# Rows 128 to 179 of the inverse transform two blocks at a time, and a wider spacing of Z in memory

## The chip, the cores and the metric

The kernel runs on one core of a Trainium2 chip. The metric is device time in microseconds (us), lower is better. A run's time is that of the whole program; the profiler recorded one execution.

## The reference

Inputs are x of shape [8, 5696, 128], a filter h of [5696, 128], complex mode weights w_r + i w_i of [64, 128, 128] and w_ch of [128, 128], all float32. A causal long convolution is followed by a mixing of the lowest 64 modes and a small pointwise layer:

```python
L = 2 * S
a = irfft(rfft(x, n=L, axis=1) * rfft(h, n=L, axis=0), n=L, axis=1)[:, :S]   # convolution
X = rfft(a, axis=1)
Y = zeros_like(X)
Y[:, :64] = einsum('bmd,mde->bme', X[:, :64], w_r + 1j * w_i)                # mode mixing
u = a + irfft(Y, n=S, axis=1)
out = u + maximum(u @ w_ch, 0)
```

## The kernel before

The transform of length 2S is split as time = 64 q + p, with 89 values of q (NQ) and 64 of p (J), and 90 frequency classes k (NK). Batches are taken in pairs, g = 0 to 3.

**First part, per pair.** A first transform over q fills As; then come "ticks" of four classes each (`tick`, NT = 23 a pair). A tick multiplies As with the matrix M (`second`, matmuls on 64 rows that alternate between partitions 0-63 and 64-127, one for each batch), multiplies by the filter's spectrum Hs (U), transforms back over the 64 points with Wc, and evacuates the result Z into Zs or Zt. From there SyncE writes Z to a scratch tensor in memory, `zscr` (512 bytes a packet, ring "z"). Matmuls of Z with G sum the modes on the side.

**Last part.** For each pair of batches Z comes back from memory with (k, real or imaginary) on the partitions: 180 rows. A block is 16 of the 64 positions p, so there are 4 blocks a pair of batches and 16 in all, numbered i. `load_zt(i)` makes two DMAs of a block: rows 0-127 into buffer ZT..a, rows 128-179 (52 of them) into ZT..b, where they stand on partitions 32-83; `clear_zt` sets partitions 0-31 of that buffer to zero on GpSimd. There are five such buffer pairs (NC = 5), laid over memory that the first part no longer uses, and block i+5 is loaded when block i has been used up. The first four blocks are loaded from within the last pair's ticks, by the table `early`.

`u_tile(i, b, half)` makes 8 positions of one batch b in two PSUM banks. For each bank there is one matmul of the mixed modes (`u_c`, IBs with C, 356 columns) and for each of 4 positions two matmuls of 89 columns, S4a with ZT..a on 128 rows and S4b with ZT..b on 84 rows. S4a and S4b are tables of cosines and sines; only half of each is loaded, and `reflect` fills the rest from it (S4a on VectorE, S4b on ScalarE). ScalarE or VectorE then copies the two banks into u (UT).

`o_tile` makes 512 output rows a time: four matmuls of u with WI = [w_ch, identity], a RELU by ScalarE into R, an addition by VectorE into an output buffer (O, 7 buffers that hold two tiles each, and 4 small ones, Os), and a DMA to the output by SyncE (ring "o"). u-tiles and o-tiles share four pairs of PSUM banks in turn (LSLOT). The loops interleave them: for the first pair of batches there are u-tiles alone, for later ones 1 and 2 o-tiles of the earlier pair after the u-tiles in turn; in the last pair all of batch 0 comes before batch 1, with 2 or 3 o-tiles after each u-tile.

Before C is known, some u-tiles of block 0 are begun "ahead" (`u_z(..., alone=True)`), between the parts of the mode mixing `mix`.

Every engine works its instructions in the order in which they are recorded; waits are derived from the buffers. All DMAs of the last part except two small ones are issued by SyncE, so a load that must wait for its buffer holds up what SyncE has after it.

Of the kernel before, what the change touches and what calls it, by code (L numbers as in the profile page):

```python
# [4 lines left out]
P = 128  # L5
# [118 lines left out]
def bass_long_conv_fft__then__afno_spectral_mix_kernel(nc, x, h, moe_w_r, moe_w_i, moe_w_ch, out):  # L124
# [3 lines left out]
    J = 64  # L128
# [33 lines left out]
    s4t = np.zeros((P, 2 * SH))  # L162
    s4t[:, 0:SH] = rows[0:P, 0:SH]
    s4t[PB:PB + RB, SH:2 * SH] = rows[P:2 * NK, 0:SH]
    sg = np.ones((P, 3))
    sr = np.stack([(-1.0) ** kk, -(-1.0) ** kk], axis=1).reshape(2 * NK)
    sg[:, 0] = sr[0:P]
    sg[PB:PB + RB, 1] = sr[P:2 * NK]
    sg[M:P, 2] = -1.0
    tt = np.arange(S)  # L170
# [79 lines left out]
    wc_sb = at("Wc", 2 * P, F16, take(2 * P * 2))  # L250
    sg_sb = at("SG", 3, F32, take(12))
# [4 lines left out]
    ZB = 16  # L256
# [4 lines left out]
    zt_off = [(a_h, a_h2), (a_as1, a_as1 + 2 * ZP), (a_as1 + 4 * ZP, a_as1 + 6 * ZP), (a_h + 2 * ZP, a_h2 + 2 * ZP),  # L261
              (a_m2, a_g)]
    assert 2 * S + 8 * ZP <= AW * 2
    zt = [[at(f"ZT{i}{'ab'[p_]}", ZP, F16, zt_off[i][p_]) for p_ in range(2)] for i in range(NC)]
    ib_sb = at("IBs", S, F16, a_m)
    s4_sb = [at("S4a", S, F16, a_m + 2 * S), at("S4b", S, F16, a_as)]
    assert 4 * S + 2 * ZP + 4 * P + 2048 <= 2 * MW
# [259 lines left out]
    ZX = [("zs", i, b) for i in range(NZ, NZL) for b in range(2)]  # L527
    zt_old = [(H_ALL, H_ALL), (AST, AST), (AST, AST), (H_ALL, H_ALL), (M_ALL[3:6], G_ALL)]

    def load_zt(i):  # L530
        g_, c_ = divmod(i, J // ZB)
        for part, (p0, r0, n) in enumerate(((0, 0, P), (PB, P, RB))):
            old = list(once(("zt", i % NC, part), zt_old[i % NC][part]))
            dma("sync", bass.AP(zt[i % NC][part], p0 * ZP, [[ZP, n], [1, ZP]]),
                bass.AP(zs, (g_ * 2 * NK + r0) * J * 256 + c_ * ZB * 256, [[J * 256, n], [1, ZP]]),
                "t", [("zd", g_, s_) for s_ in range(NT)], [("zt", i % NC, part)], after=old)

    def clear_zt(i):
        z32 = zt[i][1][0:PB, :].bitcast(U32)
        R.add("gpsimd", lambda e: e.memset(z32, 0), (), [("zt0", i)], after=list(zt_old[i][1]) + pace)  # L540

    def load_ib():
# [11 lines left out]
    def load_s4(part):  # L554
        n = PB + RB if part else P
        dma("sync", s4_sb[part][0:n, 0:SH], bass.AP(c_s4, part * SH, [[2 * SH, n], [1, SH]]), "p", (),
            [("s4", part, 0)], after=AST if part else M_ALL[1:4])
# [5 lines left out]
    early = {3: lambda: load_w(2), 5: lambda: load_w(3), 8: lambda: load_s4(1),  # L563
             9: lambda: clear_zt(0),
             10: lambda: load_zt(0),
             12: lambda: load_s4(0),
             14: lambda: (load_id(), load_ib(), clear_zt(1)),
             16: lambda: load_zt(1),
             19: lambda: (load_zt(3), clear_zt(3)),
             NT - 2: lambda: (load_zt(2), clear_zt(2))}  # L570
    pace = []

# [91 lines left out]
    def tick(g_, t):  # L664
# [27 lines left out]
        if LC <= t < NT + LC:  # L692
            s_ = t - LC
            n = len(ticks[s_])
            i, zi = s_ % NU, zroom(g_, s_)
            zb = [turns("z", ZBANK) for b in range(2)]
            for b in range(2):
                for r in range(2):
                    mm(pv(zb[b], 0, [[1, n * D]]), (W1, W2)[r], u_s[i][:, r * 1024 + b * 512:r * 1024 + b * 512 + n * D],
                       r == 0, r == 1, [("u", i), ("wc",)], [bank(zb[b])])  # L700
                evac(bass.AP(z_s[zi], b * D, [[1024, P], [2 * D, n], [1, D]]),
                     pv(zb[b], 0, [[D, n], [1, D]]), [bank(zb[b])], [("zs", zi, b)], eng="scalar",
                     after=once(("zx", zi, b), Z_OLD) if zi >= NZ else ())
                if b == 0:
                    drained(g_, t, 0)
            zo = (g_ * NK + KT * s_) * P * 256
            dma("sync", bass.AP(zs, zo, [[256, P], [P * 256, n], [1, 256]]),
                bass.AP(z_s[zi], 0, [[1024, P], [256, n], [1, 256]]), "z",
                [("zs", zi, 0), ("zs", zi, 1)], [("zd", g_, s_)])
# [39 lines left out]
    for g_ in range(NP):  # L749
# [3 lines left out]
        for t in range(NT + LM):  # L753
            tick(g_, t)
            assert g_ + 1 < NP or not wp
            if g_ == NP - 1 and t in early:
                pace[:] = [("u", min(t, NT - 1) % NU)]
                early[t]()
# [13 lines left out]

    pace[:] = []
    load_wi()
    for i in range(4, NC):
        load_zt(i)
        clear_zt(i)

# [4 lines left out]

    def u_z(i, b, half, alone=False, parts=(0, 1)):
        g_, c_ = divmod(i, NCH)
        t = ahead.get((i, b, half))
        if t is None:
            t = turns("l", LSLOT)
        z = zt[i % NC]
        for hb in parts:  # L790
            if not alone:
                u_c(i, b, half, t, hb, True)
            for pl in range(4):
                for ri in range(2):
                    pz = half * 8 + hb * 4 + pl
                    so = (c_ * ZB + pz) * NQ
                    n = (P, PB + RB)[ri]
                    mm(pv(t + hb, pl * NQ, [[1, NQ]]), z[ri][0:n, pz * 256 + b * P:pz * 256 + b * P + P], s4_sb[ri][0:n, so:so + NQ],
                       alone and pl == 0 and ri == 0, not alone and pl == 3 and ri == 1, [("zt", i % NC, ri), ("zt0", i % NC), ("s4", ri, 0)] + ([("s4", ri, 1)] if c_ >= NCH // 2 else []), [bank(t + hb)])
        if alone:  # L800
            ahead[(i, b, half)] = t
        return t

    def u_c(i, b, half, t, hb, first_):
        g_, c_ = divmod(i, NCH)
        pl0 = half * 8 + hb * 4
        mm(pv(t + hb, 0, [[1, 4 * NQ]]), c_sb[:, (2 * g_ + b) * P:(2 * g_ + b + 1) * P],
           ib_sb[:, (c_ * ZB + pl0) * NQ:(c_ * ZB + pl0 + 4) * NQ], first_, not first_,
           [("c", g_ // 2), ("ib", 0)] + ([("ib", 1)] if c_ >= NCH // 2 else []), [bank(t + hb)])

    def u_tile(i, b, half):
        g_, c_ = divmod(i, NCH)
        t = ahead.get((i, b, half))
        if t is None:
            t = u_z(i, b, half)
        else:
            for hb in range(2):
                u_c(i, b, half, t, hb, False)
        ub = (g_ % 2) * 2 + b
# [3 lines left out]
        src = pv(t, 0, [[1, NQ], [512, 2], [NQ, 4]])  # L823
        evac(bass.AP(u_sb[ub], c_ * ZB + half * 8, [[S, P], [J, NQ], [4, 2], [1, 4]]),
             src, [bank(t), bank(t + 1)], [("u_", ub, 2 * c_ + half)], eng=e, after=once(("u", ub), old))
# [32 lines left out]
    reflect("vector", ib_sb, P, 2, ("ib",), M_ALL[0:2])  # L858

# [52 lines left out]
    todo = []  # L912
    NB = NCH * NP
    NW4 = NW // 4
    for g_ in range(NP):
        last = g_ == NP - 1
        order = [(c_, b) for b in range(2) for c_ in range(NCH)] if last else [(c_, b) for c_ in range(NCH) for b in range(2)]
        for n, (c_, b) in enumerate(order):
            i = NCH * g_ + c_
            for half in range(2):  # L920
                u_tile(i, b, half)
                for _ in range((2, 2 + half)[n >= NCH] if last else 1 + half):
# [4 lines left out]
            if last and n == NCH - 1:  # L927
                todo += [(g_, 0, r4) for r4 in range(NW4)]
# [37 lines left out]
```

## Time and profile before

| | |
|---|---|
| median of 3 runs | 372.04 us (370.41 to 372.57) |
| span of the profiled execution, first to last instruction | 370.1 us |
| TensorE (PE) busy | 354.7 us, 96% |
| ScalarE (ACT) busy | 316.2 us, 85% |
| VectorE (DVE) busy | 291.8 us, 79% |
| GpSimd (POOL) busy | 75.2 us, 20% |
| granted TensorE clock | 0.999 |
| moved by DMA | 103.94 MB |

The profiled execution's own time is told by its span; the runs' times include what lies around that. In the profile a line of the grouping gives engine, operation, what is written and read, shapes and count, then busy time, the mean of one in ns, and idle time before it. L323 is the helper through which all matmuls pass, L320 that of all DMAs, so that groups are told apart by their tiles. Matmuls are pipelined: the duration of one is longer than the step from one to the next.

### The profile page before, as it was taken

The numbers are of one execution on the slowest core, as the hardware profiler recorded it, in microseconds if no ns is written. First come the engines' busy times: TensorE is split into PE (matmuls) and PEld (weight loads), VectorE is DVE, ScalarE is ACT, GpSimd is POOL, SyncE is SP. The second block draws the span as 40 slices with busy tenths as digits, with TensorE's granted clock in tenths as the row PEclk, the third lists the DMA queues.
The fourth block names the chain that finished last, engine by engine and source line by source line (L and its number), as shares of the span: only waits on it lengthen the run. The fifth ranks groups of instructions, "written<-read, shape, count | busy, mean of one in ns | idle before, by whom it ended". The sixth has DMA issues, their size and how long they took to land.

```text
span 370.1 us, 12455 instructions
## 1 busy us (share of the span) xinstructions
PE 354.7 (96%) x5350; PEld 276.5 (75%) x5350; DVE 291.8 (79%) x332; ACT 316.2 (85%) x499; POOL 75.2 (20%) x117
## 2 busy tenths in 40 slices
PE   7999899999999999999999999999999999999994
PEld 7878766667866668866668766668899888888873
DVE  3549899988999999989999988775357777756666
ACT  8559999999999999999999999995467777688885
POOL 8804012100833311823213001151000000000000
PEclk9999999999999999999999999999999999999999
DMA  7999979969999996999996999999999999999878
GB/s 139 209 271 382 249 165 292 232 198 283 93 140 213 263 258 186 132 160 215 263 278 128 171 310 363 342 345 388 381 410 386 413 410 408 418 399 376 326 291 349
DMA packets 87048, 103.94 MB, mean 281 GB/s; under 512 B 22730, under 2 KB 72522, under 8 KB 83438
## 3 DMA queue, kind: packets, MB, share of 16 engines
q1 hardware_dynamic: 64610, 81.33, 62.5%
q0 software_dynamic: 22384, 21.83, 35.4%
q8 instruction: 42, 0.69, 0.7%
q14 instruction: 12, 0.10, 0.1%
HBM read 70.61 MB, written 51.12 MB: 329 GB/s over the span
## 4 chain that ended last, share of the span: by engine, by line
PE 78%; ACT 10%; DMA 7%; DVE 3%; issue 1%; POOL 1%; DVEq 0%; POOLq 0%
PE ps L323 78%; ACT As L313 6%; DMA out_dram<-O 5%; DMA Hin<-in_h_dram 2%; ACT R L898 1%; DVE As L317 1%; ACT Xs L311 1%; DVE U L623 1%; POOL Hin L320 1%; ACT UT L311 1%; DVE O L899 0%; ACT Zs L311 0%; DVE Hp L438 0%; ACT C L313 0%; DVE Hs L315 0%
## 5 line engine op out<-in xcount | busy, mean ns | idle before, releaser
L652 DVE TENSOR_TENSOR U<-Xs,Hs 128x2048 f16<-128x2048 f16 (+1 forms) x72 | 85.8, 1197 | 12.1 <-ACT Xs L311 11.5
L323 PE MATMUL ps<-U,Wc 128*128 128x512 f16 (+1 forms) x368 | 93.8, 376 | 1.4 <-DVE U L623 1.4
L311 ACT CAST Xs<-ps 128x1024 f16<-128x1024 f32 (+1 forms) x76 | 75.0, 995 | 5.8 <-PE ps L323 3.1
L311 ACT CAST Zs<-ps 128x512 f16<-128x512 f32 (+1 forms) x132 | 70.1, 605 | 0.7
L899 DVE TENSOR_TENSOR O<-ps,R 128x512 f32<-128x512 f32 x81 | 52.4, 684 | 21.6 <-ACT R L898 11.4
L898 ACT ACTIVATE R<-ps 128x512 f32<-128x512 f32 (+1 forms) x92 | 50.5, 592 | 8.5 <-PE ps L323 8.4
L317 DVE TENSOR_SCALAR As<-ps 128x720 f16<-128x720 f32 x64 | 53.1, 879 | 4.8 <-PE ps L323 3.3
L323 PE MATMUL ps<-As,M 64*128 64x128 f16 (+3 forms) x1504 | 52.5, 214 | 2.4 <-ACT As L313 1.2
L313 ACT ACTIVATE As<-ps 128x720 f16<-128x720 f32 (+1 forms) x68 | 48.2, 771 | 5.0 <-PE ps L323 4.8
L323 PE MATMUL ps<-F,Xin 128*128 128x180 f16 x512 | 52.1, 249 | 0.1
L323 PE MATMUL ps<-WI,UT 128*128 128x256 f16 x360 | 50.8, 278 | 0.5 <-ACT UT L311 0.4
L311 ACT CAST UT<-ps 128x712 f16<-128x712 f32 x46 | 34.5, 752 | 19.4 <-PE ps L323 18.4
L323 PEld LDWEIGHTS ps<-U,Wc 128*128 128x128 f16 x368 | 29.1, 97 | 28.2 <-DVE U L623 1.9
L323 PEld LDWEIGHTS ps<-F,Xin 128*128 128x128 f16 x512 | 45.2, 155 | 6.7 <-DVE Xin L365 0.9
L323 PEld LDWEIGHTS ps<-As,M 64*128 64x128 f16 x1504 | 42.2, 94 | 8.7 <-ACT Xs L311 1.9
L323 PEld LDWEIGHTS ps<-WI,UT 128*128 128x128 f16 x360 | 38.9, 152 | 3.2 <-issue 1.8
L323 PE MATMUL ps<-IBs,C 128*128 128x356 f16 x128 | 39.2, 314 | 0.8 <-DVE O L899 0.7
L320 POOL DMA_DIRECT2D Xt<-in_x_dram x40 | 21.4, 540 | 76.5 <-PE ps L323 76.0
L323 PEld LDWEIGHTS ps<-G,Zs 128*128 128x128 f16 x512 | 26.1, 96 | 14.1 <-ACT Zs L311 0.2
L652 DVE TENSOR_TENSOR U<-ps,Hs 128x2048 f16<-128x2048 f32 (+1 forms) x16 | 35.5, 2216 | 0.0
L323 PE MATMUL ps<-G,Zs 128*128 128x128 f16 (+2 forms) x512 | 31.9, 192 | 0.1
L311 ACT CAST Zt<-ps 128x512 f16<-128x512 f32 x52 | 29.1, 659 | 0.0
(76 smaller groups left out, 479.4 us busy)
## 6 DMA issues: line engine op xcount, KB each, us to landing
out_dram<-O SPq DMA_DIRECT2D x39, 512.0 KB, 10.5
zscr<-Zs SPq DMA_DIRECT2D x62, 256.0 KB, 6.7
zscr<-Zt SPq DMA_DIRECT2D x26, 256.0 KB, 6.6
Xt<-in_x_dram POOLq DMA_DIRECT2D x20, 320.0 KB, 6.9
W<-wscr SPq DMA_DIRECT2D x4, 1024.0 KB, 8.5
ZT0a<-zscr SPq DMA_DIRECT2D x4, 1024.0 KB, 11.0
M<-cM POOLq DMA_DIRECT2D x5, 720.0 KB, 17.6
ZT1a<-zscr SPq DMA_DIRECT2D x3, 1024.0 KB, 11.1
```

Source lines behind the costliest of these rows:

```text
L311: R.add(e, lambda h_: h_.copy(dst, src), reads, writes, after=after)
L313: R.add(e, lambda h_: h_.activation(dst, src, COPY, scale=scale), reads, writes, after=after)
L317: R.add(e, lambda h_: h_.tensor_scalar_mul(dst, src, scale), reads, writes, after=after)
L320: R.add(eng, lambda h_: h_.dma_start(dst, src), reads, writes, ring=ring, after=after)
L323: R.add("tensor", lambda h_: h_.matmul(o, l, r, start=st, stop=sp), reads, writes)
L623: R.add("vector", lambda e: e.tensor_tensor(bass.AP(u_s[0], b * 512 + d0, [[2048, P], [1024, 2], [D, n], [1, d1 - d0]]), bass.AP(s_[0], s_ ...
L652: R.add("vector", lambda e: e.tensor_tensor(uv, src, hv, MULT), bk + [("h", t, 0), ("h", t, 1, 0), ("h", t, 1, J)], [("u", i)])
L898: R.add("scalar", lambda e: e.activation(rv, src_r, RELU), bk, [("r", i % NR)], after=once(("r", i % NR), G_ALL + XTT + [("y", 0), ("y", 1 ...
L899: R.add("vector", lambda e: e.tensor_tensor(ov, src_u, rv, ADD), bk + [("r", i % NR)], [key + (h_,)], after=once(key, old))
```

## The change

Rows 128-179 of two neighbouring blocks (2k and 2k+1) now share one buffer, ZB: the even block's on partitions 0-51, the odd block's on 64-115. S4b is laid out in the same way, for the even blocks on the lower and for the odd ones on the upper partitions, so that it has half the columns; it is loaded whole, and its reflection and the clears on GpSimd are gone. `u_tile(k, b, h4)` makes 4 positions of block 2k in one PSUM bank and the same 4 of block 2k+1 in the other. Its order is: both mode matmuls, eight matmuls on 128 rows, then eight on 52 rows that alternate between the lower and the upper partitions. There are 7 buffers for rows 0-127 (ZA) and 3 for the shared rows (ZB). Loads are issued at the end of a pair of blocks: both parts of ZB for pair k+3, then ZA for blocks 2k+7 and 2k+8. In memory the classes of Z are 69,632 bytes apart instead of 65,536. The number of matmuls, and the bytes of Z read and written, stay the same.

```diff
-    RB, PB = 2 * NK - P, 32
+    RB, PB = 2 * NK - P, 64
...
-    s4t[PB:PB + RB, SH:2 * SH] = rows[P:2 * NK, 0:SH]
+    s4b = np.zeros((P, S // 2))
+    for p0 in range(2):
+        s4b[p0 * PB:p0 * PB + RB] = rows[P:].reshape(RB, J // ZB // 2, 2, ZB * NQ)[:, :, p0].reshape(RB, S // 2)
+    s4t = np.concatenate([rows[0:P, 0:SH], s4b], axis=1)
...
-    zs = nc.dram_tensor("zscr", [NP * NK * P, 2 * D], F16, kind="Internal")
+    CS = P * 2 * D + 2048
+    zs = nc.dram_tensor("zscr", [NP * NK, CS], F16, kind="Internal")
...
-    NC = 5
+    NCA, NCB = 7, 3
...
-    def load_zt(i):
...
-    def clear_zt(i):
...
+    def load_za(i):
+        g_, c_ = divmod(i, J // ZB)
+        r_ = i % NCA
+        dma("sync", za[r_][:, :], bass.AP(zs, g_ * NK * CS + c_ * ZP, [[CS, P // 2], [J * 256, 2], [1, ZP]]),
+            "t", zdone(g_), [("za", r_)], after=once(("za", r_), za_old[r_]))
+
+    def load_zb(k):
+        r_ = k % NCB
+        for p0 in range(2):
+            g_, c_ = divmod(2 * k + p0, J // ZB)
+            n = RB - RS
+            dma("sync", bass.AP(zb_[r_], p0 * PB * ZP, [[ZP, n], [1, ZP]]),
+                bass.AP(zs, (g_ * NK + P // 2) * CS + c_ * ZP, [[CS, n // 2], [J * 256, 2], [1, ZP]]),
+                "t", zdone(g_), [("zb", r_, p0)], after=once(("zb", r_, p0), zb_old[r_]))
...
-             10: lambda: load_zt(0),
+             10: lambda: (load_za(0), load_zb(0)),
...
-             14: lambda: (load_id(), load_ib(), clear_zt(1)),
-             16: lambda: load_zt(1),
-             19: lambda: (load_zt(3), clear_zt(3)),
-             NT - 2: lambda: (load_zt(2), clear_zt(2))}
+             14: lambda: (load_id(), load_ib()),
+             16: lambda: load_za(1),
+             19: lambda: (load_za(2), load_zb(1)),
+             NT - 2: lambda: load_za(3)}
...
-    for i in range(4, NC):
-        load_zt(i)
-        clear_zt(i)
+    load_za(4)
+    load_zb(2)
+    load_za(5)
+    load_za(6)
...
+        if not alone:
+            for hb in range(2):
+                u_c(k, b, h4, t, hb, True)
+        for hb in range(2 if 0 in parts else 0):
+            z, r_ = za[(2 * k + hb) % NCA], (2 * k + hb) % NCA
             for pl in range(4):
...
+                mm(pv(t + hb, pl * NQ, [[1, NQ]]), z[:, pz * 256 + b * P:pz * 256 + b * P + P], s4_sb[0][:, so:so + NQ], ...)
+        for pl in range(4 if 1 in parts else 0):
...
+            for hb in range(2):
+                r0 = hb * PB
+                mm(pv(t + hb, pl * NQ, [[1, NQ]]), zb_[r_][r0:r0 + RB, pz * 256 + b * P:pz * 256 + b * P + P],
+                   s4_sb[1][r0:r0 + RB, so:so + NQ], ...)
...
-    reflect("scalar", s4_sb[1], PB + RB, 1, ("s4", 1), AST)
...
-            if b == 1 and i + NC < NB:
-                load_zt(i + NC)
+            if b == 1:
+                if k + NCB < NPR * NP:
+                    load_zb(k + NCB)
+                for i in (2 * k, 2 * k + 1):
+                    if i + NCA < NCH * NP:
+                        load_za(i + NCA)
```

More of the change, by code (lines that the diff above doesn't have):

```diff
@@ L250, in bass_long_conv_fft__then__afno_spectral_mix_kernel @@
     wc_sb = at("Wc", 2 * P, F16, take(2 * P * 2))
-    sg_sb = at("SG", 3, F32, take(12))
+    sg_sb = at("SG", 2, F32, take(8))
     XTW = 3 * M
@@ L260, in bass_long_conv_fft__then__afno_spectral_mix_kernel @@
     a_as1, a_m2 = a_as + 2 * S, a_m + 4 * S
-    zt_off = [(a_h, a_h2), (a_as1, a_as1 + 2 * ZP), (a_as1 + 4 * ZP, a_as1 + 6 * ZP), (a_h + 2 * ZP, a_h2 + 2 * ZP),
-              (a_m2, a_g)]
+    za_off = [a_h, a_as1, a_h + 2 * ZP, a_as1 + 4 * ZP, a_as1 + 6 * ZP, a_m2, a_g]
+    zb_off = [a_h2, a_h2 + 2 * ZP, a_as1 + 2 * ZP]
     assert 2 * S + 8 * ZP <= AW * 2
-    zt = [[at(f"ZT{i}{'ab'[p_]}", ZP, F16, zt_off[i][p_]) for p_ in range(2)] for i in range(NC)]
+    za = [at(f"ZA{i}", ZP, F16, za_off[i]) for i in range(NCA)]
+    zb_ = [at(f"ZB{i}", ZP, F16, zb_off[i]) for i in range(NCB)]
     ib_sb = at("IBs", S, F16, a_m)
-    s4_sb = [at("S4a", S, F16, a_m + 2 * S), at("S4b", S, F16, a_as)]
+    s4_sb = [at("S4a", S, F16, a_m + 2 * S), at("S4b", S // 2, F16, a_as)]
     assert 4 * S + 2 * ZP + 4 * P + 2048 <= 2 * MW
@@ L527, in bass_long_conv_fft__then__afno_spectral_mix_kernel, with zdone @@
     ZX = [("zs", i, b) for i in range(NZ, NZL) for b in range(2)]
-    zt_old = [(H_ALL, H_ALL), (AST, AST), (AST, AST), (H_ALL, H_ALL), (M_ALL[3:6], G_ALL)]
-    def load_zt(i):
-        g_, c_ = divmod(i, J // ZB)
[L532 to L536, printed above, removed]
-    def clear_zt(i):
-        z32 = zt[i][1][0:PB, :].bitcast(U32)
-        R.add("gpsimd", lambda e: e.memset(z32, 0), (), [("zt0", i)], after=list(zt_old[i][1]) + pace)
+    za_old = [H_ALL, AST, H_ALL, AST, AST, M_ALL[3:6], G_ALL]
+    zb_old = [H_ALL, H_ALL, AST]
+    def zdone(g_):
+        return [("zd", g_, s_) for s_ in range(NT)]
+    def load_za(i):
+        g_, c_ = divmod(i, J // ZB)
+        r_ = i % NCA
[9 more added lines that the diff above has]
+                "t", zdone(g_), [("zb", r_, p0)], after=once(("zb", r_, p0), zb_old[r_]))
     def load_ib():
@@ L554, in load_s4 @@
     def load_s4(part):
-        n = PB + RB if part else P
-        dma("sync", s4_sb[part][0:n, 0:SH], bass.AP(c_s4, part * SH, [[2 * SH, n], [1, SH]]), "p", (),
+        w = S // 2 if part else SH
+        dma("sync", s4_sb[part][:, 0:w], bass.AP(c_s4, part * SH, [[SH + S // 2, P], [1, w]]), "p", (),
             [("s4", part, 0)], after=AST if part else M_ALL[1:4])
@@ L782, in bass_long_conv_fft__then__afno_spectral_mix_kernel, with u_z @@
     ahead = {}
-    def u_z(i, b, half, alone=False, parts=(0, 1)):
-        g_, c_ = divmod(i, NCH)
-        t = ahead.get((i, b, half))
+    def u_z(k, b, h4, alone=False, parts=(0, 1)):
+        g_, c_ = divmod(2 * k, NCH)
+        t = ahead.get((k, b, h4))
         if t is None:
             t = turns("l", LSLOT)
[L789 to L792, printed above, removed]
-            for pl in range(4):
[L794 to L799, printed above, removed]
+        if not alone:
+            for hb in range(2):
+                u_c(k, b, h4, t, hb, True)
+        ns = [("s4", 0, 0)] + [("s4", 0, 1)] * (c_ >= NCH // 2)
+        for hb in range(2 if 0 in parts else 0):
+            z, r_ = za[(2 * k + hb) % NCA], (2 * k + hb) % NCA
+            for pl in range(4):
+                pz = h4 * 4 + pl
+                so = ((c_ + hb) * ZB + pz) * NQ
+                mm(pv(t + hb, pl * NQ, [[1, NQ]]), z[:, pz * 256 + b * P:pz * 256 + b * P + P], s4_sb[0][:, so:so + NQ],
+                   alone and pl == 0, False, [("za", r_)] + ns, [bank(t + hb)])
+        r_ = k % NCB
+        for pl in range(4 if 1 in parts else 0):
+            pz = h4 * 4 + pl
+            so = (c_ // 2 * ZB + pz) * NQ
+            for hb in range(2):
+                r0 = hb * PB
+                mm(pv(t + hb, pl * NQ, [[1, NQ]]), zb_[r_][r0:r0 + RB, pz * 256 + b * P:pz * 256 + b * P + P],
+                   s4_sb[1][r0:r0 + RB, so:so + NQ], False, not alone and pl == 3,
+                   [("zb", r_, hb), ("s4", 1, 0)], [bank(t + hb)])
@@ L800, in u_z, with u_c @@
         if alone:
-            ahead[(i, b, half)] = t
+            ahead[(k, b, h4)] = t
         return t
-    def u_c(i, b, half, t, hb, first_):
-        g_, c_ = divmod(i, NCH)
-        pl0 = half * 8 + hb * 4
+    def u_c(k, b, h4, t, hb, first_):
+        g_, c_ = divmod(2 * k, NCH)
         mm(pv(t + hb, 0, [[1, 4 * NQ]]), c_sb[:, (2 * g_ + b) * P:(2 * g_ + b + 1) * P],
-           ib_sb[:, (c_ * ZB + pl0) * NQ:(c_ * ZB + pl0 + 4) * NQ], first_, not first_,
+           ib_sb[:, ((c_ + hb) * ZB + h4 * 4) * NQ:((c_ + hb) * ZB + h4 * 4 + 4) * NQ], first_, not first_,
@@ L809, in u_c, with u_tile @@
            [("c", g_ // 2), ("ib", 0)] + ([("ib", 1)] if c_ >= NCH // 2 else []), [bank(t + hb)])
-    def u_tile(i, b, half):
-        g_, c_ = divmod(i, NCH)
-        t = ahead.get((i, b, half))
+    def u_tile(k, b, h4):
+        g_, c_ = divmod(2 * k, NCH)
+        t = ahead.get((k, b, h4))
         if t is None:
-            t = u_z(i, b, half)
+            t = u_z(k, b, h4)
         else:
             for hb in range(2):
-                u_c(i, b, half, t, hb, False)
+                u_c(k, b, h4, t, hb, False)
@@ L823, in u_tile @@
         src = pv(t, 0, [[1, NQ], [512, 2], [NQ, 4]])
-        evac(bass.AP(u_sb[ub], c_ * ZB + half * 8, [[S, P], [J, NQ], [4, 2], [1, 4]]),
-             src, [bank(t), bank(t + 1)], [("u_", ub, 2 * c_ + half)], eng=e, after=once(("u", ub), old))
+        evac(bass.AP(u_sb[ub], c_ * ZB + h4 * 4, [[S, P], [J, NQ], [ZB, 2], [1, 4]]),
+             src, [bank(t), bank(t + 1)], [("u_", ub, 2 * c_ + h4)], eng=e, after=once(("u", ub), old))
     XTT = [(n, g_) for g_ in range(NP) for n in ("xt", "xtn")]
     reflect("vector", s4_sb[0], P, 0, ("s4", 0), M_ALL[1:4])
-    reflect("scalar", s4_sb[1], PB + RB, 1, ("s4", 1), AST)
     MC = 4
@@ L916, in bass_long_conv_fft__then__afno_spectral_mix_kernel @@
         last = g_ == NP - 1
-        order = [(c_, b) for b in range(2) for c_ in range(NCH)] if last else [(c_, b) for c_ in range(NCH) for b in range(2)]
+        order = [(c_, b) for b in range(2) for c_ in range(NPR)] if last else [(c_, b) for c_ in range(NPR) for b in range(2)]
         for n, (c_, b) in enumerate(order):
[L919 to L922, printed above, removed]
+            k = NPR * g_ + c_
+            for h4 in range(4):
+                u_tile(k, b, h4)
+                for _ in range((2, 2 + h4 % 2)[n >= NPR] if last else 1 + h4 % 2):
                     if todo:
                         o_tile(*todo.pop(0))
-            if b == 1 and i + NC < NB:
-                load_zt(i + NC)
-            if last and n == NCH - 1:
+            if b == 1:
[4 more added lines that the diff above has]
+                        load_za(i + NCA)
+            if last and n == NPR - 1:
                 todo += [(g_, 0, r4) for r4 in range(NW4)]
```

22 lines of the change are left out of this document (8 added, 14 removed).

## The prediction

> **What bounds the kernel now.** I read the page's head first, then the busy times of four stretches of the last stage, then the chain that ended last, then the issues and landings of single DMAs.
>
> ```profile
> span 370.1 us, 12455 instructions
> PE 354.7 (96%) x5350; PEld 276.5 (75%) x5350; DVE 291.8 (79%) x332; ACT 316.2 (85%) x499; POOL 75.2 (20%) x117
> ```
> ```profile
> core 0: us, PE busy (x) PEld busy (x) DVE busy (x) ACT busy (x) POOL busy (x), PEclk, DMA share, GB/s
> 257.80:270.80 13.00, 12.97 (x239) 11.33 (x236) 4.78 (x6) 6.39 (x10) 0.00 (x0) 1.00 1.00 389
> 270.80:297.20 26.40, 26.40 (x381) 23.71 (x379) 19.00 (x28) 19.40 (x34) 0.00 (x0) 1.00 1.00 402
> 297.20:323.90 26.70, 26.43 (x378) 23.59 (x375) 19.31 (x29) 19.11 (x34) 0.00 (x0) 1.00 1.02 411
> 323.90:340.30 16.40, 15.81 (x209) 13.86 (x208) 9.64 (x16) 13.55 (x25) 0.00 (x0) 1.00 0.96 389
> ```
>
> The change touches only what begins when the last group of ticks ends (about 249 us); the windows start with the first tile that has all its operands. Two resources are full at once there. TensorE is busy 96 to 100% of each stretch, and up to 323.9 us the DMA engines are full too, at 389 to 411 GB/s. In one group of two batches the queue moves four blocks of Z (180 rows of 8 KB each, 5.9 MB) and 5.83 MB of output: 11.7 MB, 28.5 us at 411 GB/s, while the second and the third stretch, one group each, lasted 26.4 and 26.7 us. So the queue falls behind by about 2 us a group, and lives on the Z blocks that were fetched before output began.
>
> ```profile
> 262.63 54.98 PE ps L323 x816
> ...
> 320.68 16.68 DMA out_dram<-O
> ...
> 337.48 0.70 DVE O L899
> ...
> 338.32 7.48 PE ps L323 x100
> ```
> ```profile
> out_dram<-O SPq DMA_DIRECT2D x2, 512.0 KB, 12.4
> ...
> out_dram<-O SPq DMA_DIRECT2D x1, 512.0 KB, 15.6
> ```
>
> The chain is PE for 55 us, and then, once, a DMA: the output write issued at 320.68 lands 16.68 us later, VectorE at 337.48 fills the buffer that it frees, PE goes on at 338.32. The DMA view shows how that grew: 12.4 us from issue to landing for the writes issued in 297 to 304 us, 15.6 for that in 311 to 315, then the 16.68 of the chain. An output buffer can thus be away for about 16.7 us; beyond that PE waits one for one. The Z loads have as little slack there:
>
> ```profile
> 335.77 0.20 PE L323 MATMUL ps<-S4a,ZT0a 128*128 128x89 f16 x1
> 336.13 0.21 PE L323 MATMUL ps<-S4b,ZT0b 84*128 84x89 f16 x1 [0.16 <-DMA ZT0b<-zscr]
> ```
>
> Two neighbouring matmuls of block 15 start 0.36 us apart, the second released by the landing of ZT0b: a wait of 0.3 us.
>
> **PE: pairs and what frames them.**
>
> ```profile
> 257.82 0.31 PE L323 MATMUL ps<-IBs,C 128*128 128x356 f16 x1
> ...
> 258.31 0.32 PE L323 MATMUL ps<-IBs,C 128*128 128x356 f16 x1
> 258.47 0.20 PE L323 MATMUL ps<-S4a,ZT1a 128*128 128x89 f16 x1
> 258.51 0.20 PE L323 MATMUL ps<-S4b,ZT1b 84*128 84x89 f16 x1
> ```
>
> Half a u-tile before is one IBs matmul and eight Z matmuls, and the next IBs starts 0.49 us later. The IBs takes 0.16 of it (258.31 to 258.47), a Z matmul 0.04: (0.49 - 0.16) / 8 = 0.042. A whole tile, 2 IBs and 16 Z matmuls, is 0.98 us. In the changed kernel eight of the sixteen contract 52 rows, on partitions 0-51 and 64-115 in turn. The trace has such pairs already: As,M matmuls on 64 rows, which alternate between the halves.
>
> ```profile
> 225.38 0.49 PE L323 MATMUL ps<-G,Zt 128*128 128x2 f16 x8
> 225.80 1.07 PE L323 MATMUL ps<-As,M 64*128 64x128 f16 x32
> 226.80 1.04 PE L323 MATMUL ps<-U,Wc 128*128 128x512 f16 x4
> ```
> ```profile
> L323 PE MATMUL ps<-U,Wc 128*128 128x512 f16 x352 | 91.4, 381 | 1.4 <-DVE U L623 1.4
> ...
> L323 PE MATMUL ps<-As,M 64*128 64x128 f16 x1376 | 48.8, 217 | 0.5 <-ACT Xs L311 0.5
> ...
> L323 PE MATMUL ps<-G,Zt 128*128 128x128 f16 x104 | 11.3, 217 | 0.0
> ```
>
> 32 of them fill 225.80 to 226.87; the last is 0.217 long (mean ns of the form), so it began at 226.65, and fifteen pair steps took 0.85: 0.057 a pair. A single 128-row matmul of 512 columns takes (1.04 - 0.381) / 3 = 0.22 (mean of one in the grouping by form: 381 ns), a quarter of that for 128 columns is 0.055. So two halves do run in the time of one, and a pair of 89 columns should take about the 0.042 of one. But each border costs. The next 128-row matmul starts at 226.80, 0.15 after the last half where 0.057 was due: 0.09. On the way in, the last G matmul (0.217 long, its row ends at 225.87) began at 225.65 and the first As at 225.80: again 0.15 for 0.055, 0.09 more.
>
> [...]
>
> New tile: 2 x 0.16 + 8 x 0.042 + 4 x 0.042 + 2 x 0.09 = 1.00 us against 0.98 to 0.99 from the same pieces. What four pairs save (0.17) the two borders take (0.18). Over 64 tiles that is +0.6 with these roundings; with borders of 0.08 it is -0.6, with 0.10 +1.9. I take **+0.8 us**.
>
> **The queue: the same bytes, earlier.** Before, at the end of block n SP issues block n+5 (both parts). After, at the end of a pair (blocks 2k, 2k+1) it issues four DMAs together: both halves of pair k+3, that is the 52-row parts up to block 2k+7, and 128-row parts 2k+7 and 2k+8. Before, at that point, everything up to 2k+6 was out. So two 128-row parts (2.10 MB) and one 52-row part (0.43 MB) more stand ahead of the next output write: 2.53 MB at 0.41 MB/us, 6.2 us. In the middle of a pair the old kernel issues one more block and the lead falls to one 128-row part, 2.6 us. Only the end of the stage cuts it off: nothing is left after block 15.
>
> ```profile
> 311.89 0.90 SPq L320 DMA_DIRECT2D ZT4a<-zscr  x1
> 318.66 0.88 SPq L320 DMA_DIRECT2D ZT0a<-zscr  x1
> ```
>
> At the end of block 9 the old kernel issues block 14 (311.89) and block 15 at 318.66; the new one has issued all of them by the end of pair 4, at the place of 311.89: one block ahead, 1.47 MB or 3.6 us. Now add to the old latencies: after pair 3 (297 to 304 us) 12.4 + 6.2 = 18.6, after pair 4 15.6 + 3.6 = 19.2. The second exceeds 16.7 by 2.5 us. Who waits: VectorE's add for the output, behind it the PSUM pair and so PE. Two corrections. S4b is now a full 128 x 2848 table, 0.73 MB for 0.49 (84 x 2937), 0.24 MB or 0.6 us more in front of a queue that never runs empty again. And PE's own +0.8 delays the writes and so shortens the queue by as much: it is not added to the stall but absorbed by it. Excess: 2.5 + 0.6 - 0.8 = 2.3. The wait of 0.3 for block 15 goes, since it is loaded earlier. Sum: 0.8 + 2.3 - 0.3 = **+2.8 us**. Were the limit 15.7 or 17.7 instead of 16.7, it would be +3.8 or +1.8; if the queue never bites, only PE's +0.8 is left, less the 0.3.
>
> **The start of the stage.**
>
> ```profile
> ZT1a<-zscr SPq DMA_DIRECT2D x1, 1024.0 KB, 7.7
> ```
> ```profile
> 241.31 0.56 SPq L320 DMA_DIRECT2D ZT1a<-zscr  x1
> ...
> 249.94 1.09 PE L323 MATMUL ps<-XT,W 128*128 128x64 f16 x32 [0.21 <-issue]
> ```
> ```profile
> 249.47 2.60 ACT L550 ACTIVATE S4b<-S4b,SG 84x2759 f16<-84x2759 f16 x1
> 252.30 0.59 ACT L311 CAST Y<-ps 128x512 f16<-128x512 f32 x1 [0.24 <-PE ps L323]
> ```
>
> The first tile now needs block 1 too, as its second bank. Block 1 was issued at 241.31 and landed 7.7 us later, at 249.0, just as the ticks ended; the larger S4b (0.6 us) and the second half of pair 0 (0.43 MB, 1.0 us) now stand before it: up to 250.6. The mix, which follows that tile, began at 249.94, after a gap of 0.21: a delay of 0.7 to 1 us, absorbed like PE's own. Bounds 0 and +1.5; I count nothing.
>
> **At nothing.** The reflection of S4b, 2.60 us on ScalarE, goes; it ended at 252.07 and the next ScalarE instruction still waited 0.24 for PE, so it hid behind the mix, and nothing follows earlier. The five clears on GpSimd go; no matmul waits for them. u is written in runs of four elements instead of eight; the As evacuations write such runs, and their matmuls do not wait longer for it; 0 to +0.5. The stride of 69,632 bytes changes no size of any packet. Old reads at 32,768 bytes already keep the queue at 402 to 411 GB/s with the engines full, so an engine has nothing to wait less for: 0, down to -1 if a few slow reads vanish.
>
> Time: the profiled execution had a span of 370.1, so 372.9 for it; the median of the three runs is 372.04, 1.9 above that span, and I put the 2.8 on it: **374.8 us**.
>
> **Rivals.** *Only PE counts* (0.15): output buffers bear a longer absence than 16.7 us, because PSUM has four pairs of banks in turn. Against it: at 16.7 the chain already passes through the write. PE's +0.8 and the late block 1 stay, less 0.3 to 0.8 of waits: 372.5.
>
> *The border is hidden* (0.17, the other side): a 52-row weight load may slip under the 128-row matmuls before it, so that the switch shrinks below 0.04 us. [...] Then each tile is 0.1 to 0.17 shorter. As the queue is full up to 340 us, that gains there only what it lacked in waits (0.8) if the lead of the loads is absorbed as well, and 8 to 16 tiles of the last group at 0.17, 1.4 to 2.7: together -2.4, 369.6. For it: the two borders measured carry other operands. Against it: both are 0.09, in and out. It decides below 0.04.
>
> *The change does not do what it says* (0.08): 52-row matmuls follow each other like the old ones, 0.042 each, and still pay the borders: 64 x 4 x 0.042 = +10.8 on PE, in which the queue's stall is absorbed: 372.04 + 0.8 + 10.8 = 383.6. The As pairs speak against it.
>
> **Numbers.** The queue case has 0.60. About 0.5% (1.9 us) is what a measurement of this kernel can tell from no change. Of the 0.60, 0.48 lies above +1.9 and 0.10 below, 0.02 under zero with a faster DMA. Slower 0.48 + 0.08 = 0.56; same 0.10 + 0.15 + 0.01 = 0.26; faster 0.16 + 0.02 = 0.18. The queue case alone reaches from 372.9 to 376.5. The range takes in the hidden border below (368.5) and above a queue limit of 15.7 with a late block 1 (378.0); left out are the serial pairs and the rest of the tails, under 0.2.
>
> **What would show it.** Right: pairs of S4b matmuls that start nearly together, with 0.15 us between the last S4a and the first of them; output writes that take 17 to 19 us to land around 300 to 325 us; one or a few PE waits on VectorE's add near 325 us, 2 us or more in all; no wait for Z blocks 12 to 15; stretches of a group 26.5 to 27 us where no wait falls. Wrong: a u-tile without o-tiles of 0.90 us or less (border hidden), or of 1.15 (serial pairs); output latencies under 16 us throughout; a DMA rate of 425 GB/s or more in the stretches that had 402 to 411 (then the stride does count).

## The result and the profile after

The changed kernel takes 388.0 us (median of 4 runs, 386.56 to 389.83), the kernel before 371.9 (370.41 to 372.57): a ratio of 1.043, 95% interval 1.039 to 1.048. Predicted were 374.8, in a range from 368.5 to 378.0. The sign was right, the size was not: the loss is 16 us where 2.8 was expected. The profiled execution after, the run of 389.83, has a span of 388.0 (370.1 before).

The page's head, after:

```profile
span 388.0 us, 12443 instructions
PE 363.0 (94%) x5350; PEld 275.1 (71%) x5350; DVE 291.2 (75%) x332; ACT 314.4 (81%) x498; POOL 66.8 (17%) x112
```

The busy times of the same four stretches as in the prediction, after:

```profile
257.80:270.80 13.00, 12.30 (x236) 10.59 (x234) 3.67 (x5) 3.37 (x5) 0.00 (x0) 0.78 1.03 336
270.80:297.20 26.40, 26.33 (x411) 21.03 (x408) 14.17 (x20) 15.71 (x26) 0.00 (x0) 1.00 1.01 347
297.20:323.90 26.70, 24.92 (x330) 20.22 (x327) 17.37 (x26) 16.77 (x30) 0.00 (x0) 0.94 0.99 386
323.90:340.30 16.40, 13.83 (x171) 11.13 (x170) 8.86 (x13) 8.79 (x16) 0.00 (x0) 0.90 1.00 380
```

Read the last two columns together. The DMA engines are as full as before (0.99 to 1.03), and yet move 336 and 347 GB/s where they moved 389 and 402. Busy all the time and moving less, they had slower packets or smaller ones, not more waiting; the packet records below say slower (the 8 KB packets that started in 250 to 340 us took 367 ns at the mean, 320 before). The column before them is the granted clock: 0.78, 0.94 and 0.90 in three of the four stretches, where it was 1.00.

The chain that ended last, after, from the end of the ticks:

```profile
248.21 9.02 DMA ZA<-zscr
257.27 7.98 PE ps L326 x164
...
269.63 12.12 DMA ZA<-zscr
...
286.04 16.99 DMA out_dram<-O
303.14 0.70 DVE O L912
303.98 12.27 PE ps L326 x153
316.82 17.35 DMA out_dram<-O
334.30 0.70 DVE O L912
```

Before, one output write stood in it after 55 us of PE; now a load of block 1, a later load and two output writes of 17 us do. The groups of the first matmul of a u-tile, and of those that read ZA, say how long PE waited (the first line before, the others after):

```profile
L323 PE MATMUL ps<-IBs,C 128*128 128x356 f16 x128 | 39.2, 314 | 0.8 <-DVE O L899 0.7
L326 PE MATMUL ps<-S4a,ZA 128*128 128x89 f16 x512 | 33.6, 209 | 2.4 <-DMA ZA<-zscr 2.3
L326 PE MATMUL ps<-IBs,C 128*128 128x356 f16 x128 | 30.4, 323 | 4.6 <-DVE O L912 4.4 <-ACT C L316 0.2
```

So 4.4 us on output buffers (0.7 before) and 2.3 on ZA. They are three waits: 2.3 us up to 257.3, 1.8 up to 304.0 and 2.6 up to 335.1. At each of them TensorE ran at half clock for some us, which shows as 0.83 in the slices that hold it (after, 10 us each):

```profile
250.00:260.00 10.00, 7.03 (x100) 5.10 (x97) 3.49 (x4) 3.91 (x9) 0.47 (x1) 0.83 1.08 372
260.00:270.00 10.00, 9.30 (x179) 7.92 (x178) 3.05 (x5) 2.69 (x4) 0.00 (x0) 0.83 1.02 310
300.00:310.00 10.00, 8.22 (x96) 6.40 (x95) 5.38 (x9) 4.51 (x9) 0.00 (x0) 0.83 1.03 398
330.00:340.00 10.00, 7.43 (x80) 5.76 (x79) 4.79 (x8) 3.88 (x7) 0.00 (x0) 0.83 1.00 386
```

0.83 in 10 us is 3.4 us at half clock: 6.8 us at the first wait, 3.4 at each of the others, which cost up to 6.8 us more in all. (Some 4 us more of this one execution were lost at 70 to 80 us, where copies of Hs landed late. In that stretch PE is busy 7.21 us here and 9.99 before, but also 9.06 in experiment 1 and 7.43 in 10, whose first parts are alike, and I don't count it to the change.)

Where the time went can be read at one matmul that has the same place in both orders, the first of the o-tiles: it starts at 271.3 before and at 282.3 after. So 11 of the 18 us between the two profiles were lost before any output was written: 5.6 of them up to the last matmul of the ticks (U with Wc), among them the 4 at 70 to 80 us, and 5.4 at the start of the stage, around the wait for block 1. The two waits for output buffers and the half clock behind them make the rest.

### The profile page after: what moved, and what is told of

Read it like the earlier page. It is cut to its first block, busy times and chain, and to the rows that moved or that the text cites. A ratio compares the mean times of both kernels' runs of the same rounds, so it can differ in the third digit from the quotient of the medians.

```text
span 388.0 us, 12443 instructions
## 1 busy us (share of the span) xinstructions
PE 363.0 (94%) x5350; PEld 275.1 (71%) x5350; DVE 291.2 (75%) x332; ACT 314.4 (81%) x498; POOL 66.8 (17%) x112
## 4 chain that ended last, share of the span: by engine, by line
PE 60%; DMA 20%; ACT 10%; DVE 5%; issue 2%; SPq 1%; POOL 1%; DVEq 0%; POOLq 0%
PE ps L326 60%; DMA out_dram<-O 9%; ACT As L316 6%; DMA ZA<-zscr 5%; DMA Xt<-in_x_dram 2%; DMA Hin<-in_h_dram 2%; ACT Xs L314 2%; DMA Hs<-Hs 2%; DVE As L320 1%; ACT R L911 1%; SPq L323 1%; DVE Hs L318 1%; DVE O L912 1%; DVE U L630 1%; POOL Hin L323 1%
## 5 line engine op out<-in xcount | busy, mean ns | idle before, releaser
L326 PE MATMUL ps<-U,Wc 128*128 128x512 f16 (+1 forms) x368 | 94.8, 379 | 1.9 <-DVE U L630 1.4
L326 PE MATMUL ps<-WI,UT 128*128 128x256 f16 x360 | 52.8, 285 | 0.7 <-issue 0.3
L326 PEld LDWEIGHTS ps<-S4a,ZA 128*128 128x128 f16 x512 | 29.7, 101 | 9.8 <-DMA ZA<-zscr 2.7
L326 PE MATMUL ps<-S4a,ZA 128*128 128x89 f16 x512 | 33.6, 209 | 2.4 <-DMA ZA<-zscr 2.3
L326 PE MATMUL ps<-IBs,C 128*128 128x356 f16 x128 | 30.4, 323 | 4.6 <-DVE O L912 4.4
```

The lines of the kernel that those rows point to most:

```text
L326: R.add("tensor", lambda h_: h_.matmul(o, l, r, start=st, stop=sp), reads, writes)
```

## The experiments

The numbers are those of the labels; there is no 6. All have their own runs of the kernel before beside them (371.7 to 372.7). For most I show the window from 260 to 300 us, for some also that from 300 to 330. The kernel before, with the columns:

```profile
core 0: us, PE busy (x) PEld busy (x) DVE busy (x) ACT busy (x) POOL busy (x), PEclk, DMA share, GB/s
260.00:300.00 40.00, 39.97 (x615) 35.74 (x613) 24.52 (x35) 26.00 (x43) 0.00 (x0) 1.00 1.01 401
300.00:330.00 30.00, 29.62 (x414) 26.24 (x413) 20.51 (x31) 22.70 (x40) 0.00 (x0) 1.00 1.01 410
```

**1 and 2: the spacing.** From the changed kernel, spacing back:

```diff
-    CS = P * 2 * D + 2048
+    CS = P * 2 * D
```

> The changed kernel with the classes of Z 65,536 bytes apart again, all else the same. If the wider spacing slows the copies of Hs in the ticks or the reads of Z (the stretches from 260 to 300 us moved 310 to 375 GB/s where the kernel before moved 389 to 411), this run takes 372 to 380 us and those stretches go back to 390 or more. If the arrangement alone is the cause (the order of the loads, the early need of block 1, the borders on PE, and the clock that is halved after each idle spell), it takes 385 to 389 us.

And the spacing alone, in the kernel before (the writes of Z likewise):

```diff
+    CS = P * 2 * D + 2048
...
-                bass.AP(zs, (g_ * 2 * NK + r0) * J * 256 + c_ * ZB * 256, [[J * 256, n], [1, ZP]]),
+                bass.AP(zs, (g_ * NK + r0 // 2) * CS + c_ * ZP, [[CS, n // 2], [J * 256, 2], [1, ZP]]),
```

> The kernel before with only the spacing of the classes changed to 69,632 bytes. If the spacing is a cause, 376 us or more and a lower DMA rate in the last stage; if not, 371 to 373 us.

Measured: 387.9 us (385.56 to 391.76) and 373.0 (371.91 to 374.07, ratio 1.002, 0.999 to 1.005). The windows of the first, and of the second:

```profile
260.00:300.00 40.00, 37.06 (x562) 29.39 (x562) 21.43 (x31) 22.80 (x36) 0.00 (x0) 1.00 1.01 363
```
```profile
260.00:300.00 40.00, 40.00 (x625) 35.72 (x624) 24.46 (x35) 26.48 (x43) 0.00 (x0) 1.00 1.00 390
```

The spacing is not the cause, in either direction.

**3 and 4: the order of the loads.** Both at a spacing of 65,536.

```diff
-             12: lambda: load_s4(0),
+             12: lambda: (load_za(1), load_s4(0)),
...
-             16: lambda: load_za(1),
```

> As e1_stride_64k, but block 1's rows 0-127 are issued at tick 12, ahead of S4a, not at tick 16. If the late block 1 costs its wait of 2.5 us and half of the 6.8 us at half clock behind it, this run is 3 to 6 us below e1_stride_64k. If what is gained there is only absorbed by the queue's later stalls, it is within 1.5 us of e1_stride_64k and the two waits for output buffers grow.

```diff
-            if b == 1:
...
+            i = 2 * k + 5 + b
+            if i < NCH * NP and not last:
+                load_za(i)
+                load_zb(i // 2, (i % 2,))
```

> As e1_stride_64k, but the loads go out in the cadence of the kernel before: one block (both parts) after each block's worth of u-tiles, and never more than five blocks ahead. If the bunched loads that run ahead are what makes the two writes of output land after 17 us, the waits of 1.95 and 2.74 us on the output buffers and the two stretches of 3.4 us at half clock go: 6 to 9 us below e1_stride_64k. If the waits come from the queue being slower in whatever order, within 2 us of e1_stride_64k.

Measured: 388.8 (384.84 to 389.97) and 392.2 (390.4 to 395.07). Neither brought a gain. Experiment 3 stayed within 1.5 us of experiment 1, as its second branch said; experiment 4 was 4 us slower than experiment 1, which neither branch had. Without its lead the kernel is slower, and its rate is the lowest so far (experiment 4):

```profile
260.00:300.00 40.00, 35.00 (x506) 27.35 (x501) 18.02 (x26) 20.59 (x32) 0.00 (x0) 0.91 0.99 313
```

So the loads themselves are slow, in whatever order. In the packet records of the traces an 8 KB packet takes 309 ns at the median, before and here. But in experiment 1 there are spells, around the time when loads of the shared rows land, in which nearly all are slow: of the 81 that started in 269 to 272 us, 78 took 500 to 640 ns.

**5: only the place of rows 128-179.** The kernel before, one number changed:

```diff
-    RB, PB = 2 * NK - P, 32
+    RB, PB = 2 * NK - P, 64
```

> New theory, since neither the spacing nor the order nor the lead of the loads brought the time back: a load of 52 rows is slow when all its partitions lie in one half of the 128 (0-51 or 64-115), and was fast on 32-83, which takes 32 of one half and 20 of the other. The packets of 8 KB took 309 ns each but about twice that while a load of the shared rows was in flight. This kernel is the one before with a single number changed: rows 128-179 stand on partitions 64-115 instead of 32-83 (the zeros below them on 0-63, contraction over 116 rows instead of 84, the table S4b 116 rows). No pairs, no borders, the old order of loads, spacing 65,536. By the theory each of the 16 loads takes about 1.2 us longer on its engines, up to 12 us of that while the queue is full: 378 to 386 us, and 310 to 380 GB/s in the stretches that had 389 to 411. If the halves don't matter: 371 to 374 us.

Measured: 398.7 us (397.05 to 402.45), ratio 1.074 (1.068 to 1.081), more than was expected.

```profile
260.00:300.00 40.00, 35.83 (x535) 31.52 (x536) 19.52 (x28) 21.55 (x34) 0.00 (x0) 0.96 1.01 301
300.00:330.00 30.00, 26.62 (x340) 23.02 (x336) 17.81 (x27) 17.34 (x30) 0.00 (x0) 0.89 1.00 353
```

The old kernel, with none of the change but the partitions, loses more than the changed kernel. (Part of it may be S4b, whose 116 rows landed only after 13.5 us; in experiments 9 and 10 it landed after 7.7 and 7.8.)

**7 and 8: two tries to load both halves at once.** One load of 128 rows, both blocks' rows in it; and the odd halves on GpSimd's queue.

```diff
+        dma("sync", zb_[r_][:, :],
+            bass.AP(zs, (g_ * NK + P // 2 - RE // 2) * CS + c_ * ZP, [[ZP, 2], [J * 256, PB], [1, ZP]]), ...)
```

> As e1_stride_64k, but both blocks' shared rows come by one DMA over all 128 partitions: 64 rows a block, 12 of them rows 116-127 again, for which S4b holds zeros; the pairs contract 64 rows. 1.57 MB more to read, 3.8 us of the queue at 411 GB/s. By the theory of the halves the rate goes back to 390 or more and the time to 372 to 378 us, with PE's 2 us and a part of the 3.8 left. If the pairs, the order or something else slows the queue, 386 to 392 us.

```diff
-            dma("sync", bass.AP(zb_[r_], p0 * PB * ZP
+            dma("gpsimd" if p0 and k else "sync", bass.AP(zb_[r_], p0 * PB * ZP
```

> As e1_stride_64k, but the odd blocks' shared rows are issued by GpSimd on its own queue, so that the two halves can be in flight at once. If the half is a limit that the two loads don't share, they overlap: 374 to 381 us. If loads of the two queues follow each other on the engines all the same, 384 to 390 us.

Measured: 524.4 (522.39 to 525.79) and 393.5 (392.99 to 398.85). The first is slow for a reason of its own:

```profile
300.00:330.00 30.00, 11.92 (x164) 8.49 (x161) 3.58 (x5) 4.36 (x6) 0.00 (x0) 0.67 0.44 153
```

Share 0.44: the 16 DMA engines were idle for more than half of the time. Between 310 and 320 us the share was 0.13, two sixteenths, at 54 GB/s, and the landing of each of these loads of 1 MB stepped its semaphore twice, where that of a load of ZA steps it sixteen times. I read this as two engines at work; the slowest dimension of the source is 2 here, the two blocks. In the second run another queue didn't help (393.5 us, 387.9 in experiment 1).

**9, 10 and 12: other partitions, and another split of the rows.** The kernel before with rows 128-179 from partition 44, and from 60 (the same one number as in experiment 5):

> The kernel before with rows 128-179 on partitions 44-95 instead of 32-83: 20 of the 52 in the lower half of the partitions, 32 in the upper (32 and 20 before). In e5_before_p64 the table S4b came in 116 rows and took 13.5 us to land instead of 8; here it has 96 rows, which go evenly on 16 engines. If only a load that puts more than 32 of its 52 rows into one half is slow, this is the kernel before: 370 to 374 us. If any move away from 32-83 costs, above 378.

> As e9_before_p44, on partitions 60-111: 4 rows in the lower half and 48 in the upper; S4b has 112 rows, again even on 16 engines. By the theory of the halves the packets of these loads take about 500 to 600 ns instead of 309, and the time is 380 to 398 us, 310 to 380 GB/s. If e5_before_p64 was slow for its late S4b or its larger contraction: 371 to 376 us.

Measured: 393.4 (390.72 to 394.99) and 397.1 (393.37 to 402.95). From 44, rows lie in both halves, 20 and 32, and it is slow all the same:

```profile
260.00:300.00 40.00, 33.38 (x517) 29.21 (x514) 17.82 (x26) 21.52 (x35) 0.00 (x0) 0.99 1.01 276
```

My theory of the halves fell with this. What was left to try was how the rows are shared out among the engines. The last of the three keeps partitions and bytes and changes only that:

```diff
+            for m, n_ in ((0, n),) if part == 0 else ((0, 48), (48, n - 48)):
+                dma("sync", bass.AP(zt[i % NC][part], (p0 + m) * ZP, [[ZP, n_], [1, ZP]]), ...)
```

> The theory of the halves fell with e9_before_p44. New theory: what counts is which of the 16 DMA engines writes which partitions. [...] This kernel is the one before with rows 128-179 on the same partitions 32-83, the same bytes, but each load of 52 rows is made as two, 48 rows (three an engine on 16 engines) and 4 rows. By the theory of the engines 380 to 398 us and packets of 500 to 600 ns; if the set of partitions is what counts, 371 to 374 us.

Measured: 385.7 (381.17 to 390.29).

```profile
260.00:300.00 40.00, 35.26 (x525) 30.91 (x522) 19.52 (x27) 21.88 (x35) 0.00 (x0) 0.96 1.02 286
300.00:330.00 30.00, 26.89 (x363) 23.40 (x361) 19.72 (x29) 18.46 (x32) 0.00 (x0) 0.97 1.02 403
```

The same 52 rows on the same partitions 32-83, issued as 48 and 4, cost 13.6 us at the median (the lowest of its times, 381.17, is 7.8 above the highest of the kernel before, 373.35) and take the rate from 401 to 286 GB/s. There are 16 loads more, but at a share of 1.02 the engines did not lack work. So the place alone doesn't decide, the split counts too. Experiments 5, 9 and 10 are the other half: there the rows are read from the same addresses by loads of the same shape, and only the partitions that they go to differ. Here the two together decided.

Why is not in the trace, which doesn't say which engine carried a packet. What it shows is how often a load's landing steps its semaphore: sixteen times for 128 or 48 rows, fourteen for the 84 rows of S4b before, thirteen for 52, four for the 4 rows of experiment 12. I read a step as one engine, so that 52 rows are four on each of thirteen engines and 48 three on each of sixteen; the two steps and two sixteenths in experiment 7 agree with it. By this reading both the split and the place change which engine writes which partition, which was the theory of experiment 12, and its 385.7 us lie in the range of that theory. It stays a guess, since no run shows which engine wrote which partition. In packets (8 KB, started in 250 to 340 us):

| kernel | rows of a load, steps of its semaphore | mean packet, ns | GB/s in 260-300 | median, us |
|---|---|---|---|---|
| before, from 32 | 52, thirteen | 320 | 401 | 372 |
| changed, from 0 and from 64 | 52 and 52, thirteen each | 367 | 342 | 388.0 |
| 5, from 64 | 52, thirteen | 415 | 301 | 398.7 |
| 12, from 32 | 48, sixteen, and 4, four | 419 | 286 | 385.7 |
| 9, from 44 | 52, thirteen | 432 | 276 | 393.4 |
| 10, from 60 | 52, thirteen | 451 | 263 | 397.1 |
| 15, rows 52-179, from 0 | 128, sixteen | 317 | 411 | 377.4 |

Small steps of the table mean nothing: experiments 1, 3, 4 and 8, whose loads have the rows and places of the changed kernel's, have means of 360, 379, 398 and 394 ns. But the groups stay apart: 317 to 331 ns with 52 rows from 32 or 128 rows from 0 (experiments 2, 11, 13 and 14 too), 360 to 398 with 52 rows from 0 and from 64, and 415 and more with 52 rows from 44, from 60 or all from 64, or with 48 and 4 from 32. (The medians hold more than the rate, what each kernel's S4b costs for one; row 10 has a span of 401.2 us, above its median.) It is not only the loads of the 52 rows that are slow: in experiment 9 all 445 packets of 8 KB that started in 268 to 284 us took 481 ns or more, those of 128-row loads too. How the packets are slowed stays open.

**11, 13, 14 and 15: the change with loads of 128 rows.** The changed kernel, spacing 69,632, with one load of 128 rows a pair:

```diff
+        dma("sync", zb_[r_][:, :],
+            bass.AP(zs, (g_ * NK + RB // 2) * CS + c_ * ZP, [[CS, P // 2], [J * 256, 2], [1, ZP]]), ...)
```

> The changed kernel itself, spacing 69,632 and all, but the two loads of a pair's shared rows are replaced by one load of 128 rows (52 to 179 of the even block) over all 128 partitions, split like the loads of ZA; the odd block's own rows 128-179 are left out, and the pairs contract what lies on partitions 0-51 and 64-115. 1.57 MB more to read. If the halves are the cause, the rate in the last stage is 390 GB/s or more and the time 372 to 379 us: what then is left over the kernel before is PE's borders (2 us), the lead of the loads (2.3 us at most as predicted), the late block 1 and some of the extra bytes. If the pairs or the order matter for the queue: 385 us or more.

> The kernel of e11_after_zb_even again, for a second profile: 375 to 378 us.

Both leave out the odd blocks' own rows 128-179, so they show a time and are no kernel to use; so do the next two. Measured: 376.7 (374.38 to 381.92), and again 377.4 (376.7 to 378.32, ratio 1.014, 1.010 to 1.018). Of the 16 us, 11 are gone, with pairs, order, lead, spacing and early block 1 all as in the changed kernel, and 1.57 MB more to read. Experiment 15, windows, waits and chain:

```profile
260.00:300.00 40.00, 39.95 (x600) 32.14 (x599) 24.54 (x34) 25.15 (x40) 0.00 (x0) 1.00 1.02 411
300.00:330.00 30.00, 28.58 (x400) 23.40 (x399) 20.23 (x31) 20.48 (x36) 0.00 (x0) 1.00 1.02 419
```
```profile
L326 PE MATMUL ps<-IBs,C 128*128 128x356 f16 x128 | 29.4, 315 | 1.7 <-DVE O L911 1.4 <-ACT C L316 0.2
```
```profile
261.62 44.04 PE ps L326 x662
305.82 16.62 DMA out_dram<-O
322.56 0.70 DVE O L911
323.39 28.24 PE ps L326 x378
```

Then the same without the lead of the loads (cadence as in experiment 4), and without the need of block 1 in the first tiles:

> As e11_after_zb_even, but the loads go out in the old cadence (ZA one block at a time, five blocks ahead, the pair's load with the even block), without the lead of two ZA. If the lead still costs in e11_after_zb_even what was predicted for it, this is 2 us faster, 372 to 375 us; if the queue, once it runs at 418 to 425 GB/s, has room for the lead, the same within 1 us; if the lead helps, slower, with waits for ZA or ZB.

```diff
-            z, r_ = za[(2 * k + hb) % NCA], (2 * k + hb) % NCA
+            z, r_ = za[(2 * k + hb * (k > 0)) % NCA], (2 * k + hb * (k > 0)) % NCA
```

> As e11_after_zb_even, but the first pair's tiles read block 0's rows 0-127 for both banks, so that the first tile no longer needs block 1 (which is still loaded); block 1's rows 0-127 are left out of the result. If the wait for block 1 and the halved clock behind it make the rest of the loss, 2 to 4 us below e15_even_again (372 to 375 us). If the queue or PE takes the gain back later, within 1 us of it.

Measured: 378.9 (376.27 to 380.44) and 376.8 (376.32 to 377.5). Without the lead no wait for an output buffer is left (experiment 13),

```profile
L326 PE MATMUL ps<-S4a,ZA 128*128 128x89 f16 x512 | 32.6, 205 | 4.2 <-DMA ZA<-zscr 4.2
L326 PE MATMUL ps<-IBs,C 128*128 128x356 f16 x128 | 29.4, 315 | 0.3 <-ACT C L316 0.2
```

and still the time doesn't fall. The 4.2 us on ZA say nothing of the lead: 3.8 of them are the wait for block 1 in the first tile, up to 255.65, and block 1 had been issued at 245.03, before the lead begins (242.37 in experiment 15). What the lead costs at the full rate is thus not measured. Without the need of block 1 the early wait is nearly gone (0.5 us on ZA, 1.2 in experiment 15) and comes back as waits for output buffers (2.6 us for 1.4): 0.6 us faster, which can't be told from nothing. What was gained at the start was lost again in the waits for output.

## Why the prediction was wrong, step by step

*What bounds the kernel*: right. PE (96 to 100% busy before) and the queue (a share of 1.00 to 1.02 up to 323.9 us) are both full, which is why slower packets cost time at all.

*PE, pairs and borders*: right in kind, a little small. A u-tile after:

```profile
270.93 0.47 PE L326 MATMUL ps<-IBs,C 128*128 128x356 f16 x2
271.24 0.50 PE L326 MATMUL ps<-S4a,ZA 128*128 128x89 f16 x8
271.67 0.34 PE L326 MATMUL ps<-S4b,ZB 52*128 52x89 f16 x8
271.94 0.33 PE L326 MATMUL ps<-IBs,C 128*128 128x356 f16 x1
```

The last S4a begins at 271.24 + 0.50 - 0.21 = 271.53, the first S4b 0.14 later (0.15 was expected); eight S4b and the way out take 0.27. The tile is 1.01 us, predicted 1.00, before 0.98: 64 x 0.03 = 1.9 us for the 0.8 that I took, at the upper bound of that step. The rivals of a hidden border and of serial pairs are both out.

*The queue, "the same bytes, earlier"*: the step that failed. It divided the bytes ahead by 0.41 MB/us, the old rate, and so took for granted that the new loads run like the old ones. I had written that rows 128-179 move from partitions 32-83 to 0-51 and 64-115, and priced the clears and S4b for it, but not the load's own speed; of the changes in the loads I weighed only the spacing. The rate fell to 342 GB/s, and 11 of the 16 us went with one load of 128 rows a pair (experiments 11 and 15). Two signs that I had named for being right, output writes of 17 us or more and waits of about 2 us behind them, were there and came from this other cause.

The limit of 16.7 us for an output buffer was too high as well. In experiment 15, at the old rate or above, the write that stops PE took 16.62 us, where 19.2 was predicted, and PE still waited 1.4 us up to 323.4: there the buffers bore about 15.2. Before, behind the write of 16.68 from which I read the limit, PE had already waited 0.3. The 1.4 us come near the predicted 2.3 near 325 because two errors offset each other, which is luck. In experiment 13, without the lead, no output buffer was waited for, as that step has it.

*The start of the stage*: "I count nothing" was wrong for what is seen: a wait of 2.3 us for block 1 with 6.8 us at half clock, 5.4 us lost there in the profile, beyond the bound of 1.5. What it costs in the end isn't settled. Experiment 3 moved block 1 forward and gained nothing, but there matmuls of the last ticks waited 3.8 us for ScalarE's Zs instead. Experiment 14 does without block 1, but at the full rate, where the wait was only 1.2 us: it gained nothing that can be measured.

*At nothing*: the spacing is worth nothing, as counted (experiments 1 and 2). The granted clock was not in the sum at all: in the changed kernel each wait of 1.8 us or more from 20 us on came with 3.4 us or more at half clock.

What is left of experiment 15 over the kernel before, 4.8 us, would be PE's 1.9 and 1.81 MB more than before (105.75 for 103.94 MB) in a full queue, 4.4 us at 411 GB/s, which overlap. No run took the two apart. In its profile most of the loss is early: the first matmul of the o-tiles starts 3.9 us later than before (275.1 for 271.3), of which 0.9 were lost up to the last matmul of the ticks and 1.2 in the wait for block 1, with 3.4 us at half clock behind it. A load at the old rate that brings the rows of both blocks and reads none twice wasn't found: with both blocks' rows in one load the source's slowest dimension is 2, and in experiment 7 that ran at a share of 0.44 and 153 GB/s.

## What to carry to other kernels

Before moving a load to other partitions or splitting its rows anew, measure its rate in a run that changes nothing else; bytes and packet size alone don't give it: here the row count of a load and the partition at which it starts decided between 401 GB/s and 263. When the DMA share stays at 1.0 and the GB/s fall, look at the packets of one size: if they have become slower, as here (367 ns for 320), reordering the queue may not be the remedy; two other orders (388.8 and 392.2 us) and a second queue (393.5) gained nothing on 387.9. A constant like 32 that seems to be chosen for convenience deserves a test by itself: one number brought more than the whole loss to the old kernel (398.7 us for 371.8).

## What the runs showed that was not expected

Loads of the same 52 rows on the same partitions ran at 401 or 286 GB/s in the same stretch, for nothing but being issued as 52 or as 48 and 4 rows. A load whose source had 2 as its slowest dimension left the engines at a share of 0.44. And waits of 1.8 to 2.6 us, in experiment 15 one of 1.2, came with 3.4 us or more at half clock; before, with waits of up to 0.5 us from 20 us on, the clock stayed at 1.00. The length alone doesn't decide: in experiment 9 a wait of 3.1 us (332 to 335 us) left it at 1.00.
